# Two spectrum products in one VectorE instruction, and two of seven inverse-stage evictions moved to VectorE

## The chip, the cores and the metric

The kernel runs on one core of a Trainium2 chip. The metric is the device time of one execution in microseconds (us). The core has a matrix engine (TensorE, PE in the profile; its weight loads are PEld), VectorE (DVE), ScalarE (ACT), GpSimd (POOL) and SyncE (SP), which here only issues DMAs. All engines run their own instruction lists in order and meet through semaphores.

## The reference, cut to what matters

The input is a sequence batch x of shape (8, 5696, 128) and a filter h of shape (5696, 128). First comes a causal long convolution along the sequence, done through a Fourier transform of twice the length; then a mixing block over tokens and channels.

```
L = 2 * S
Yf = np.fft.rfft(x, n=L, axis=1) * np.fft.rfft(h, n=L, axis=0)[None]
y = np.fft.irfft(Yf, n=L, axis=1)[:, :S]
theta = y @ w_theta
z = (y * cos(theta), y * sin(theta))
u = y + y_from(w_tok_r, z[0]) + y_from(w_tok_i, z[1])
out = u + relu(u @ w_ch)
```

The change touches only the convolution.

## The kernel before, in words

The convolution occupies the first fifth of the execution; the token mixing, two 5696 x 5696 matrices against the rotated values, fills the rest and keeps TensorE busy almost without a gap (line 1099).

A transform of length 11392 is split into 64 x 178 points, of which 90 columns are kept because the input is real. The work is cut into eight groups, four pairs of batches times two halves of 64 channels. A group passes through four stages.

- **Stage a** (`stage_a`, matmul on line 194) makes the 90 columns in 16 steps; ScalarE evicts each step from PSUM (line 201; 128 x 720).
- **Stage b** (`stage_b`) goes over the 90 columns in 12 chunks, eleven of 8 columns and one of 2. For a chunk, `f2` does 32 short matmuls into a PSUM tile (line 212), ScalarE evicts it as the spectrum tile `xs` (line 310; 128 x 1024), and VectorE multiplies `xs` by the two rows of the filter's spectrum `hs`, one instruction for each (line 312), into `u_t` and `v_t`. The pool of `xs` has two buffers, so the eviction of chunk c waits until the products of chunk c-2 have read theirs. The tile `hs` of chunk c comes from DRAM in two DMAs on SP's queue (line 303); the pool has four buffers, and the loads of chunk c+4 are issued behind the products of chunk c (`LEAD = 4`). The last chunk's PSUM tile also takes 12 wide matmuls that only keep TensorE busy (line 218).
- **Stage c** (`stage_c`) is matmuls of `u_t` and `v_t` against two small tables (lines 328 and 329), which need all chunks of stage b; VectorE (line 336) and for some steps ScalarE (lines 333 and 334) evict them into `g`.
- **Stage d** (`stage_d`) is the last inverse transform: seven steps of up to ten columns, 20 matmuls for a full step (line 351), each evicted by ScalarE into `yt` (line 354; 128 x 890, the last one 128 x 356). Its first step needs all of `g`. At its end `yt` goes to DRAM.

The order of the work is written by hand with `woven`, which merges lists of steps by fractional positions. Two stretches alternate. In one, stage c of a group is woven with stage a of the next. In the other, stage b of the next group is woven with stage d of this one; I call it the **b/d stretch**, and there are seven of it. Its order of steps is b0 d0 b1 b2 d1 b3 b4 d2 b5 b6 d3 b7 d4 b8 b9 d5 b10 b11 d6. In front of the seven there is one stage b without a stage d (about 68 to 88 us), woven with the building of a table, and behind them one stage d without a stage b (about 422 to 438 us), woven with the first steps of the mixing part (`phase_step`), which use ScalarE for sines. All convolution matmuls share a pool of four PSUM tiles, so TensorE can be at most four steps ahead of the evictions. Four steps of the following stage a stand on TensorE between the end of a b/d stretch and the first matmul of stage c. A scheduler places the instructions of each engine; with one exception, noted with the change, it keeps the written order around here.

Of the kernel before, what the change touches and what calls it, by code (L numbers as in the profile page):

```python
# [12 lines left out]
F16 = mybir.dt.float16  # L13
add = mybir.AluOpType.add
mult = mybir.AluOpType.mult
AF = mybir.ActivationFunctionType
# [6 lines left out]
def kernel(  # L23
# [10 lines left out]
    nc = tc.nc  # L34
    B, S, D = x.shape
    assert D == 128
    P = 128
# [42 lines left out]
    K1 = N1 // 2 + 1  # L80
    CK = 8
    HD = D // 2
# [5 lines left out]
    CN = 10  # L88
    CHN = [(c0, min(CN, N2 - c0)) for c0 in range(0, N2, CN)]
    UVW = 2 * HD * K1  # L90
# [6 lines left out]
    def psum():  # L97
        return fp.tile([P, 2, 512], F32, tag="ps", name="ps")
# [3 lines left out]
    def pool(name, bufs, stack, **kw):  # L102
        return stack.enter_context(tc.tile_pool(name=name, bufs=bufs, **kw))
# [6 lines left out]
    fc = pool("fft_c", 1, conv, side="right")  # L110
# [1 line left out]
    s1 = pool("set_1", 1, setup, side="right")  # L112
    s2 = pool("set_2", 2, setup, side="right")

    u_t = fc.tile([P, UVW + P], F16)
    v_t = fc.tile([P, UVW + P], F16)
    uv = [t[:, :UVW].rearrange("p (e d k) -> p e d k", e=2, k=K1) for t in (u_t, v_t)]
    h16 = s1.tile([P, 2, N2, HD], F16)
    for p0, p1 in ((0, 80), (80, NB)):
        nc.gpsimd.dma_start(u_t[p0:p1, :N2 * D],  # L120
# [22 lines left out]
    def turns_of(pattern, base, lanes, m, per, quarter=None):  # L143

        n = 1
        for _, c in pattern:
            n *= c
        t = s2.tile([P, 11 * NB], F32, tag="turn", name="turn")[:m, :n]
        k = s2.tile([P, 11 * NB], F32, tag="whole", name="whole")[:m, :n]
        nc.gpsimd.iota(k, pattern=pattern, base=base, channel_multiplier=0,  # L150
                       allow_small_or_imprecise_dtypes=True)
        nc.gpsimd.tensor_scalar(t, k, lanes, 1.0 / per, op0=mult, op1=mult)
        if quarter is not None:
            quarter(t)
        nc.vector.tensor_scalar(k, t, MAGIC, None, op0=add)
        nc.vector.scalar_tensor_tensor(t, k, MAGIC, t, op0=ALU.subtract, op1=ALU.subtract)
        return t, k
# [12 lines left out]
    t, k = turns_of([[1, K1]], 0, lane[:NB, 1:2], NB, N1)  # L170
# [33 lines left out]
    def f2(a_st, c):  # L204

        c0, ck = CHK[c]
        ps = psum()
        for j in range(ck):
            for ri in range(2):
                for e in range(2):  # L210
                    rows = slice(64 * e, 64 * e + 64)
                    nc.tensor.matmul(ps[:, e, j * HD:(j + 1) * HD],  # L212
                                     w_t2[rows, c0 + j, N2 * (1 - ri):N2 * (3 - ri)],
                                     a_st["a"][rows, ri * K1 + c0 + j, :],
                                     start=(ri == 0), stop=(ri == 1))
        if c == NCK - 1:
            for n in range(WARM):
                nc.tensor.matmul(ps[:, n % 2, ck * HD:ck * HD + 384], w_t2[:, 2, :P],
                                 w_t2[:, 0:2, :].rearrange("p k n -> p (k n)"), start=True, stop=True)
        return ps[:, :, :ck * HD].rearrange("p e (k d) -> p e d k", k=ck)  # L220
# [73 lines left out]
    def stage_b(a_st, dh):  # L294

        hs_of = {}

        def load(c):
            if c >= NCK:
                return  # L300
            hs = hs_of[c] = fh.tile([P, 2, HD * CK], F16, tag="hs", name="hs")
            for e in range(2):
                nc.sync.dma_start(hs[64 * e:64 * e + 64], hf_hbm[dh, c])

        def chunk(c):
            c0, ck = CHK[c]
            hv = hs_of[c].rearrange("p r (d k) -> p r d k", k=CK)
            ps = f2(a_st, c)
            xs = fs.tile([P, 2, HD, CK], F16, tag="xs", name="xs")
            nc.scalar.activation(xs[:, :, :, :ck], ps, AF.Copy)  # L310
            for r in range(2):
                nc.vector.tensor_tensor(  # L312
                    uv[r][:, :, :, c0:c0 + ck], xs[:, :, :, :ck],
                    hv[:, r:r + 1, :, :ck].to_broadcast([P, 2, HD, ck]), op=mult)
            load(c + LEAD)
        return [lambda c=c: load(c) for c in range(LEAD)], [lambda c=c: chunk(c) for c in range(NCK)]

# [21 lines left out]
    def stage_d(st, bp, dh, then=None):  # L339
        def chunk(n0, cn):  # L340
            if n0 == 0:
                st["yt"] = fg.tile([P, NB, N2], BF16, tag="yt", name="yt")
            g_, yt = st["g"], st["yt"]
            ps = psum()
            nq = 5 if cn == CN else cn
            for j in range(cn):
                n = n0 + j
                o = ps[:, j // nq, (j % nq) * NB:(j % nq + 1) * NB]
                for ri in range(2):
                    e_ = e_t[:K1, n, ri, :] if n < EN else e_t[:K1, N2 - n, ri, ::-1]  # L350
                    nc.tensor.matmul(o, g_[:K1, ri * N2 + n, :], e_, start=(ri == 0), stop=(ri == 1))
            y_out = yt[:, :, n0:n0 + cn].rearrange("p m (a q) -> p m a q", q=nq)
            y_in = ps[:, :cn // nq, :nq * NB].rearrange("p a (q m) -> p m a q", q=nq)
            nc.scalar.activation(y_out, y_in, AF.Copy)
            if n0 + cn == N2:
                if then is not None:
                    then(yt)
                if then is not None:
                    gate = nc.gpsimd.tensor_copy(small(0, 1)[HD:HD + 1], sides["phases"][1][HD:HD + 1, 3, H - 1:H]).ins
                for e in range(2):  # L360
                    t0 = H if then else 0
                    with tc.issue_after(gate) if then else ExitStack():
                        (nc.gpsimd if then else nc.sync).dma_start(
                            yt_hbm[dh * HD:(dh + 1) * HD, 2 * bp + e, t0:],
                            yt[64 * e:64 * e + 64].rearrange("p m n -> p (m n)")[:, t0:])
        return [lambda n0=n0, cn=cn: chunk(n0, cn) for n0, cn in CHN]
# [125 lines left out]
    def small(at, n):  # L492
        return ring["all"][:, WB + BT + at:WB + BT + at + n]
# [436 lines left out]
    for i, (k, p, tt, j0, s0, nj) in enumerate(stretches):  # L930
# [38 lines left out]
        if tt is None:  # L969
# [24 lines left out]
            if end_of_pair:  # L994
# [5 lines left out]
                c, c0 = c_last  # L1000
# [161 lines left out]
```

## Time and profile before

| what | us |
|---|---|
| three timed runs, median (lowest to highest) | 2102.5 (2101.66 to 2104.44) |
| the profiled execution, its own time | 2099.89 |
| span of the profiled execution | 2098.1 |
| TensorE busy / VectorE busy / ScalarE busy in the span | 1979.5 / 1595.2 / 675.3 |
| mean granted TensorE clock | 0.978 |
| start of the first spectrum eviction in the seven b/d stretches | 111.05, 153.10, 195.88, 238.35, 281.18, 325.06, 369.11 |

The time of an execution is a little longer than its span, which runs from the first to the last recorded instruction (1.8 us here). Rows of the profile give start and duration of an instruction or of a merged run of equal ones; square brackets give the idle time of the engine before it and what ended that. Instructions that stand back to back overlap a little in the records, so what one costs its engine is the distance from start to start (its slot), not its duration.

### The profile page before, as it was taken

The page shows a single profiled execution, that of the slowest core. Times are in us where ns is not written, and L with a number is a line of the kernel's source. Part 1 is how long each engine was busy: PE and PEld are TensorE (multiplying, and loading weights), DVE is VectorE, ACT ScalarE, POOL GpSimd, SP SyncE. Part 2 cuts the span into 40 slices and gives each one's busy share as a digit, 9 for nine tenths or more (in the row PEclk, how much of TensorE's full clock was granted, in tenths as well). Part 3 has the DMA queues.
Part 4 walks back from the last instruction along what each step waited for, and adds up shares of the span by engine and source line. Part 5 has one row for each costly group of instructions (what it writes and reads, how often), then busy time and mean ns, then how long its engine had stood idle before and what let it go on. Part 6 is the DMA issues. An engine that isn't in the chain of part 4 may idle for free.

```text
span 2098.1 us, 41505 instructions
## 1 busy us (share of the span) xinstructions
PE 1979.5 (94%) x15688; PEld 1109.4 (53%) x15865; DVE 1595.2 (76%) x2881; ACT 675.3 (32%) x995; POOL 912.5 (43%) x1662
## 2 busy tenths in 40 slices
PE   4888999878999999999999999899999999999998
PEld 3788888754444444444444444344444444444444
DVE  7777776776878888888886766886777777777867
ACT  5887877874332333333310000011111111111111
POOL 5301010327444636354557554435354545445450
PEclk8799999989999999999999999999999999999999
DMA  7357474989989989898999989869797887879693
GB/s 144 94 137 175 123 171 121 239 243 239 179 153 179 178 175 168 171 173 177 171 175 152 154 167 284 136 107 156 127 154 132 148 142 136 154 130 155 126 155 89
DMA packets 408233, 334.97 MB, mean 160 GB/s; under 512 B 85895, under 2 KB 358407, under 8 KB 407047
## 3 DMA queue, kind: packets, MB, share of 16 engines
q0 software_dynamic: 225952, 156.72, 52.8%
q1 hardware_dynamic: 176096, 164.05, 27.3%
q10 hardware_dynamic: 5984, 11.54, 1.6%
q8 instruction: 124, 2.03, 0.4%
q14 instruction: 77, 0.63, 0.1%
HBM read 377.11 MB, written 92.49 MB: 224 GB/s over the span
## 4 chain that ended last, share of the span: by engine, by line
PE 63%; DVE 4%; DMA 2%; issue 2%; POOL 0%; ACT 0%; DVEq 0%
PE m L1099 59%; DVE c L1106 2%; DMA ring<-in_moe_w_tok_r_dram 1%; DVE b L655 1%; PE v L801 1%; PE utp L794 1%; PE m L1103 1%; DVE wt L714 1%; PE tpz L742 0%; PE theta_ps L396 0%; POOL ring L509 0%; PE m L986 0%; DMA yT<-yt_hbm 0%; PE m L1020 0%; DMA zl<-zl_hbm 0%
## 5 line engine op out<-in xcount | busy, mean ns | idle before, releaser
L509 POOL DMA_DIRECT2D ring<-in_moe_w_tok_i_dram x720 | 390.8, 557 | 653.0 <-DVE wt L714 579.6
L509 POOL DMA_DIRECT2D ring<-in_moe_w_tok_r_dram x720 | 389.0, 559 | 145.8 <-DVE wt L714 85.5
L714 DVE STREAM_TRANSPOSE wt<-ring 128x384 f32<-128x384 f32 (+2 forms) x720 | 359.3, 523 | 110.3 <-PE m L1099 70.0
L1099 PE MATMUL m<-b,wt 128*128 128x512 bf16 x1599 | 385.9, 380 | 4.1 <-DVE wt L714 1.7
L1099 PEld LDWEIGHTS <-wt 128*128 128x128 bf16 x1804 | 176.4, 98 | 219.7 <-DVE wt L714 7.8
L1106 DVE TENSOR_TENSOR c<-c,m 128x512 f32<-128x512 f32 x412 | 265.2, 669 | 0.4 <-PE m L1099 0.4
L796 ACT ACTIVATE ring<-utp 128x512 bf16<-128x512 bf16 x85 | 50.8, 597 | 582.3 <-PE utp L794 582.3
L328 PE MATMUL ps<-r_u,u_t 128*128 128x128 f16 x1024 | 126.4, 223 | 6.4 <-ACT red L419 3.0
L329 PE MATMUL ps<-r_v,v_t 128*128 128x128 f16 x1024 | 125.5, 223 | 0.4
L1020 PE MATMUL m<-b,wt 128*128 128x512 bf16 x466 | 110.2, 381 | 8.9 <-DMA b<-z_hbm 4.9
L791 ACT ACTIVATE ub<-c 128x512 bf16<-128x512 f32 x88 | 55.0, 628 | 191.5 <-DMA ring<-in_moe_w_tok_r_dram 113.0
L130 POOL DMA_DIRECT2D x<-in_x_dram x64 | 33.9, 536 | 184.9 <-PE ps L194 174.8
L328 PEld LDWEIGHTS <-u_t 128*128 128x128 f16 x1024 | 103.4, 101 | 5.5 <-DVE u_t L312 4.6
L329 PEld LDWEIGHTS <-v_t 128*128 128x128 f16 x1024 | 102.4, 100 | 4.4 <-issue 2.4
L310 ACT ACTIVATE xs<-ps 128x1024 f16<-128x1024 f32 x96 | 96.6, 1030 | 14.7 <-DVE v_t L312 6.7
L312 DVE TENSOR_TENSOR u_t<-xs,hs 128x1024 f16<-128x1024 f16 x96 | 68.6, 715 | 29.2 <-ACT xs L310 19.0
L1020 PEld LDWEIGHTS <-wt 128*128 128x128 bf16 x528 | 51.1, 99 | 69.2 <-issue 9.6
L194 PE MATMUL ps<-f_t,x 89*128 89x180 f16 x512 | 77.2, 298 | 4.0 <-ACT xs L310 2.6
L212 PEld LDWEIGHTS <-w_t 64*128 64x128 f16 x3240 | 60.8, 102 | 37.5 <-issue 24.5
L398 ACT ACTIVATE red<-theta_ps,magic 128x512 f32<-128x512 f32 (+1 forms) x46 | 31.6, 687 | 134.6 <-PE theta_ps L396 104.5
L194 PEld LDWEIGHTS <-x 89*128 89x128 f16 x512 | 70.8, 241 | 5.5 <-issue 4.5
L744 ACT ACTIVATE ring<-tpz 128x512 bf16<-128x512 bf16 (+1 forms) x46 | 27.5, 597 | 131.9 <-PE tpz L742 113.0
(2895 smaller groups left out, 3868.9 us busy)
## 6 DMA issues: line engine op xcount, KB each, us to landing
ring<-in_moe_w_tok_r_dram POOLq DMA_DIRECT2D x352, 96.0 KB, 4.5
ring<-in_moe_w_tok_i_dram POOLq DMA_DIRECT2D x352, 96.0 KB, 4.9
ring<-in_moe_w_tok_r_dram POOLq DMA_DIRECT2D x352, 80.0 KB, 4.5
ring<-in_moe_w_tok_i_dram POOLq DMA_DIRECT2D x352, 80.0 KB, 3.9
hs<-hf_hbm SPq DMA_DIRECT2D x192, 128.0 KB, 3.1
cp_hbm<-c SPq DMA_DIRECT2D x88, 256.0 KB, 2.5
c<-cp_hbm SPq DMA_DIRECT2D x88, 256.0 KB, 4.4
out_dram<-c SPq DMA_DIRECT2D x88, 256.0 KB, 4.5
```

Of the source, the lines that this page charges most:

```text
L194: nc.tensor.matmul(ps[:, i // 2, (i % 2) * 2 * K1:(i % 2 + 1) * 2 * K1], lhs(q + i), f1_t[:NB], start=True, stop=True)
L212: nc.tensor.matmul(ps[:, e, j * HD:(j + 1) * HD], w_t2[rows, c0 + j, N2 * (1 - ri):N2 * (3 - ri)], a_st["a"][rows, ri * K1 + c0 + j, :], s ...
L310: nc.scalar.activation(xs[:, :, :, :ck], ps, AF.Copy)
L312: nc.vector.tensor_tensor(uv[r][:, :, :, c0:c0 + ck], xs[:, :, :, :ck], hv[:, r:r + 1, :, :ck].to_broadcast([P, 2, HD, ck]), op=mult)
L328: nc.tensor.matmul(o, u_t[:, at:at + P], r_u, start=True, stop=False)
L329: nc.tensor.matmul(o, v_t[:, at:at + P], r_v, start=False, stop=True)
L509: nc.gpsimd.dma_start(wb[32 * i:32 * i + 32, :ng, :nj * 64], bass.AP(tensor=a.tensor, offset=a.offset + row0 * S + p * H + i * QR + j0 * 6 ...
L714: nc.vector.transpose(wt.rearrange("p j t r -> p (j t r)").bitcast(F32).rearrange("p (j g t) -> p g j t", j=TJ, g=4)[:, :ng, :nj], wb[:, : ...
L791: nc.scalar.activation(ub[:m].rearrange("p b d -> p (b d)"), c[:m], AF.Copy)
L1020: nc.tensor.matmul(ms[n // 2 * 2 + h], a[n][:, j, :, r], bts_of[p][jj][n % 2 * 2 + h][:, r, :], start=(n % 2 == 0 and jj == 0 and r == 0), ...
L1099: nc.tensor.matmul(ms[q], a[q][:, j, :, r], bts[jj][q][:, r, :], start=(jj == 0 and r == 0), stop=(jj == NJ - 1 and r == 1 and q not in left))
L1106: nc.vector.tensor_tensor(c, z, ms[q], op=op)
```

## The change

The tiles `u_t` and `v_t` become the two parts of one tile `uv_t`. For the eleven full chunks the two products become one instruction over 128 x 2 x 1024 elements: `xs` is repeated over the two parts, each row of `hs` over the two halves of the chunk. The chunk of 2 columns keeps its two instructions. In stage d, steps 1 and 4 of 0 to 6 are evicted by VectorE instead of ScalarE.

```
-    u_t = fc.tile([P, UVW + P], F16)
-    v_t = fc.tile([P, UVW + P], F16)
-    uv = [t[:, :UVW].rearrange("p (e d k) -> p e d k", e=2, k=K1) for t in (u_t, v_t)]
+    uv_t = fc.tile([P, 2, UVW + P], F16)
+    u_t, v_t = uv_t[:, 0], uv_t[:, 1]
+    uv = uv_t[:, :, :UVW].rearrange("p r (e d k) -> p r e d k", e=2, k=K1)
...
-            for r in range(2):
+            if ck == CK:
                 nc.vector.tensor_tensor(
-                    uv[r][:, :, :, c0:c0 + ck], xs[:, :, :, :ck],
-                    hv[:, r:r + 1, :, :ck].to_broadcast([P, 2, HD, ck]), op=mult)
+                    uv[:, :, :, :, c0:c0 + ck], xs.unsqueeze(1).to_broadcast([P, 2, 2, HD, ck]),
+                    hv.unsqueeze(2).to_broadcast([P, 2, 2, HD, ck]), op=mult)
+            else:
+                for r in range(2):
+                    nc.vector.tensor_tensor(
+                        uv[:, r, :, :, c0:c0 + ck], xs[:, :, :, :ck],
+                        hv[:, r:r + 1, :, :ck].to_broadcast([P, 2, HD, ck]), op=mult)
             load(c + LEAD)
...
-            nc.scalar.activation(y_out, y_in, AF.Copy)
+            if n0 // CN in (1, 4):
+                nc.vector.tensor_copy(y_out, y_in)
+            else:
+                nc.scalar.activation(y_out, y_in, AF.Copy)
```

In the built program the order on TensorE and on SP's queue within the convolution is the same as before. In a b/d stretch ScalarE's order loses the two evictions and is otherwise unchanged. VectorE's order is: products of chunks 0 and 1, eviction of step d1, products of chunks 2 to 6, eviction of step d4, products of chunks 7 to 11. The eviction of d1 is thus ahead of the product of chunk 2, although the written order has b2 ahead of d1. In the last stage d the two moved evictions stand between VectorE's products of the mixing part.

## The prediction

> **What bounds the kernel now.** I read the busy shares first, then the stretches of the convolution, then VectorE and ScalarE in one stretch in order of time, then the waits.
>
> ```profile
> PE 1979.5 (94%) x15688; PEld 1109.4 (53%) x15865; DVE 1595.2 (76%) x2881; ACT 675.3 (32%) x995; POOL 912.5 (43%) x1662
> ```
>
> TensorE is the bound of the whole. That is an average; the change sits in the b/d stretches, so here are three of them alone (the columns are stretch, its length, then busy us of PE, PEld, DVE, ACT and POOL, the granted clock, DMA share and GB/s):
>
> ```profile
> 153.20:173.00 19.80, 16.47 (x484) 14.45 (x484) 16.34 (x24) 18.12 (x22) 0.00 (x0) 1.00 0.46 137
> 238.50:258.00 19.50, 16.67 (x484) 14.56 (x484) 15.87 (x24) 17.95 (x21) 0.00 (x0) 1.00 0.47 133
> 325.00:344.00 19.00, 15.51 (x478) 13.67 (x479) 14.72 (x23) 16.50 (x19) 0.00 (x0) 1.00 0.44 128
> ```
>
> Here TensorE has 3 us of slack at full clock, ScalarE is the fullest and VectorE comes close behind. The stretch ends, and stage c begins, when VectorE's last product is done: in the second stretch the last one runs from 173.00 to 173.39 and the first matmul of stage c starts at 173.15. So what counts is how the chain ScalarE - VectorE runs, not which column is fullest. VectorE in that stretch:
>
> ```profile
> 156.80 0.70 DVE L312 TENSOR_TENSOR u_t<-xs,hs 128x1024 f16<-128x1024 f16 x1 [1.34 <-ACT xs L310]
> 157.41 0.69 DVE L312 TENSOR_TENSOR v_t<-xs,hs 128x1024 f16<-128x1024 f16 x1
> 158.01 0.69 DVE L312 TENSOR_TENSOR u_t<-xs,hs 128x1024 f16<-128x1024 f16 x1
> ...
> 167.25 0.69 DVE L312 TENSOR_TENSOR u_t<-xs,hs 128x1024 f16<-128x1024 f16 x1 [1.08 <-DMA hs<-hf_hbm]
> ```
>
> A product has a slot of 0.60 to 0.61, a pair 1.21. The last row shows the second thing that holds VectorE: the filter's spectrum, loaded only after the product four chunks earlier. The waits over 60 to 440 us (total, times, longest) put these side by side:
>
> ```profile
> DVE u_t L312 <- ACT xs L310: 19.0, 28, 1.3
> DVE u_t L312 <- DMA hs<-hf_hbm: 8.4, 11, 1.5
> ACT xs L310 <- DVE v_t L312: 6.7, 15, 1.6
> ```
>
> The third line matters most: ScalarE also waits for VectorE, through the two `xs` buffers. The two engines drive each other.
>
> **Part one, the joined products.** Two slots of 0.605 become one longer one. For f32 from PSUM the copies of 720 elements (0.895) and 1024 elements (1.215, line 246) give 1.05 ns an element and a fixed 0.14. At half that rate 1024 elements take 0.54 + 0.15 = 0.69, which is the product's row, so I read the product as running at twice that rate, and 2048 elements take 0.605 + 0.54 = 1.14. Bounds: the 128 x 256 products (slot 0.30) give a slope of 0.40 ns an element, so 1.01; no gain gives 1.21. I take 1.14, nearest to the same engine at the same rate. Saved: 0.07 a chunk, 0.8 us in eleven chunks. The price of losing the double rate is a rival below. Loads and the reuse of `xs` waited for the second product already, so the joint one frees them 0.07 earlier and no more.
>
> **Part two, the moved evictions.** ScalarE sheds two slots of 0.80, 1.6 us a stretch. VectorE gains two: 0.895 plus 170 elements at 1.05 ns is 1.07, slot 0.99, together 2.0. No row has VectorE evicting this shape; the bounds are 0.81 (720 elements) and 1.14 (1024 elements), and I take the interpolated 0.99. VectorE thus has 1.2 us more work per stretch than before.
>
> [...]
>
> **The chain of one stretch.** Times are us after the start of the first spectrum eviction (153.10 in the stretch shown). Before, from rows: the products of chunks 1, 2, 3, 4, 5 start at 3.70, 4.91, 6.33, 7.54, 9.09 (second stretch), and, in the sixth, where no DMA wait falls there, chunk 6 at 10.29 and chunk 8 at 13.44; the eviction of chunk 10 starts at 15.13 there, which puts its product at 16.2. After, step by step with spectrum slot 0.90 (1.03 to its end), product end 1.22 after its start, and 0.03 and 0.12 of hand-over to VectorE and back:
> - Chunk 1 stays at 3.70 (its eviction stands behind d0's, still on ScalarE). d1's eviction comes next on VectorE, at 4.84: its matmuls end at about 3.74.
> - Chunk 2 goes to 5.83 (0.92 late), chunk 3 to 6.97.
> - The spectrum of chunk 4 needs chunk 2's buffer: 5.83 + 1.22 + 0.12 = 7.17, product 8.23 (0.7 late). ScalarE stands idle here; the slot that it was spared is lost.
> - d2's eviction at 8.07, chunk 5's spectrum at 8.87, product at 9.93 (0.84 late); chunk 6 at 11.07.
> - d4's eviction on VectorE at 12.21, then chunks 7, 8, 9 at 13.20, 14.34 and 15.48. Chunk 8 is 0.9 late.
> - Chunk 9's spectrum needs chunk 7's buffer (14.54), then d5's eviction at 15.44, chunk 10's spectrum at 16.24, product at 17.30.
>
> So chunk 10 is 1.1 late where no load is late. Behind it things stay: the last products run beside stage a's first matmuls (line 194) in both versions and are slow beside them (1.90 instead of 0.69 at 170.28).
> - Against that stand the loads. The second DMA of a chunk is issued 0.6 us behind the first (median of the issue rows) and lands 3.1 us later (median): about 3.7 behind the product that frees the buffer, 5.0 with that product, and more when one is late. Products four chunks apart start 5.4 to 5.9 apart before, 5.2 to 6.2 after. Some late loads (8.4 us in all, 1.2 a stretch) will be covered by the slower pace, up to 0.4 a stretch I estimate.
>
> I take +0.9 a stretch, between +0.7 and +1.1; seven times, +6.3. The other ends: a product of 1.01 takes about 0.6 off a stretch (ten products, half of them covered by other waits), one of 1.21 adds 0.3: +1 to +10 in all.
>
> **Outside the seven.** The first stage b has only the joined products: -0.2 (0 to -0.8). In the last stage d ScalarE is without idle time from 429.8 to 446.9, so one moved eviction (0.79) is worth its slot, the other (before 428.15, where ScalarE waits 0.54 for VectorE) less; VectorE, busy 20.6 of 29.0 us there, pays 2.0. I take -0.5 (+0.5 to -1.6). What follows is a chain on TensorE and through data of the convolution, so it moves along.
>
> Sum: 6.3 - 0.2 - 0.5 = **+5.6 us** on the profiled execution's own time, 2099.9 to 2105.5. That execution is 2.6 below the median shown; on the median the forecast is 2108.1, rounded 2108.
>
> **Rivals.**
> - *ScalarE sets the pace (faster).* It is the fullest engine in each stretch shown, and 1.6 us are taken from it. If VectorE's new slots fall into its idle time (1.34 before chunk 1, 1.08 before chunk 8), 1.2 a stretch is gained, with the last stage -9.6: 2093. It decides if d1's and d4's evictions do not delay the next spectrum, that is if buffer waits (6.7 us in total now) stay few. Against it: d1's eviction can't start before its matmuls end, when the 1.34 gap is over.
> - *The loads hold both versions.* If late loads fall where VectorE's evictions now stand, the evictions are free and the stretch keeps its length: 0 to +0.3 each, about +1: 2103.
> - *The joined product loses its rate.* At f32's 1.05 ns, 2048 elements take 2.28, 1.07 a chunk more; 88 chunks, some 20 of it hidden: +75, 2178. Its operands keep 16 bits and unit steps inside, as before; only outer repeats change.
>
> **How the numbers follow.** Forecast 0.50 (+1 to +10 us), loads 0.30 (-2 to +4), ScalarE 0.16 (-13 to -4), lost rate 0.04. This kernel's measurement tells about 0.2%, 4.2 us, from no change. Of the forecast's case 0.45 lies over +4.2 and 0.05 within; of the loads' 0.02 over and 0.28 within; of ScalarE's 0.01 within, 0.15 below. Slower is 0.45 + 0.02 + 0.04 = 0.51, same 0.34, faster 0.15. The range leaves out the lost rate and the far part of ScalarE's case: 2095 to 2115; the likeliest case alone is 2103 to 2113.
>
> **What would show it.** Right: joined products with a slot near 1.14; VectorE's evictions near 1.07; ScalarE idle before the spectra of chunks 4 and 10, released by VectorE; stretches about 0.9 longer from first spectrum to stage c. Wrong: stretches shorter, few buffer waits of ScalarE, or products near 2.2.

## The result, and the profile after

| | before | after |
|---|---|---|
| median of 22 runs each, us (lowest to highest) | 2100.13 (2096.52 to 2105.53) | 2105.30 (2100.21 to 2115.21) |
| span of the profiled execution, us | 2098.1 | 2105.6 |

The ratio after to before is 1.0025, with a 95% interval of 1.0013 to 1.0036: the change costs 5.2 us (2.7 to 7.6). The forecast was +5.6.

The busy shares of the changed kernel (first line of the profile's page) say little by themselves. VectorE gained 10.2 us and ScalarE lost 12.6:

```profile
PE 1982.7 (94%) x15688; PEld 1112.7 (53%) x15865; DVE 1605.4 (76%) x2809; ACT 662.7 (31%) x979; POOL 907.9 (43%) x1662
```

The same three b/d stretches as before (columns as in the prediction's table of stretches; each starts at its first spectrum eviction and ends at about the first matmul of stage c; the windows in the prediction's table end 0.1, 0.4 and 1.6 us ahead of that matmul, so the lengths of the two tables cannot be compared, only what fills them):

```profile
156.40:177.20 20.80, 16.27 (x484) 14.48 (x484) 17.73 (x16) 17.19 (x20) 0.00 (x0) 1.00 0.43 130
243.00:263.50 20.50, 16.19 (x484) 14.41 (x484) 17.61 (x16) 17.04 (x20) 0.00 (x0) 1.00 0.45 131
329.40:350.00 20.60, 16.25 (x484) 14.47 (x484) 17.66 (x16) 16.95 (x20) 0.00 (x0) 0.99 0.44 130
```

TensorE is about as busy as it was, ScalarE is no longer the fullest engine, and yet a stretch takes longer (20.84, 20.55 and 20.66 us up to that matmul, against 20.04, 20.09 and 20.49). Neither VectorE nor ScalarE is full; each waits for the other. VectorE in the second stretch, whose first spectrum eviction starts at 156.39:

```profile
160.13 1.23 DVE L312 TENSOR_TENSOR uv_t<-xs,hs 128x2048 f16<-128x2048 f16 x1 [1.46 <-ACT xs L310]
161.27 1.08 DVE L360 CAST yt<-ps 128x890 bf16<-128x890 f32 x1
162.26 3.59 DVE L312 TENSOR_TENSOR uv_t<-xs,hs 128x2048 f16<-128x2048 f16 x3
166.65 2.36 DVE L312 TENSOR_TENSOR uv_t<-xs,hs 128x2048 f16<-128x2048 f16 x2 [0.80 <-DMA hs<-hf_hbm]
168.93 1.08 DVE L360 CAST yt<-ps 128x890 bf16<-128x890 f32 x1
169.92 4.15 DVE L312 TENSOR_TENSOR uv_t<-xs,hs 128x2048 f16<-128x2048 f16 x3
174.44 2.43 DVE L312 TENSOR_TENSOR uv_t<-xs,hs 128x2048 f16<-128x2048 f16 x1 [0.37 <-ACT xs L310]
```

Two slots can be read off: a joined product takes 1.14 (160.13 to 161.27), an eviction of stage d on VectorE 0.99 (161.27 to 162.26). The second row is d1's eviction: it stands where, before, the product of chunk 2 stood. ScalarE in the same stretch:

```profile
159.07 1.94 ACT L310 ACTIVATE xs<-ps 128x1024 f16<-128x1024 f32 x2
161.45 1.02 ACT L310 ACTIVATE xs<-ps 128x1024 f16<-128x1024 f32 x1 [0.44 <-DVE uv_t L312]
163.57 1.02 ACT L310 ACTIVATE xs<-ps 128x1024 f16<-128x1024 f32 x1 [1.10 <-PE ps L212]
...
171.23 1.02 ACT L310 ACTIVATE xs<-ps 128x1024 f16<-128x1024 f32 x1 [1.10 <-DVE uv_t L312]
```

The third row is the spectrum of chunk 4, 1.10 late. The profile names TensorE as its releaser, and that needs a second look: TensorE's rows put the matmuls of chunk 4 into this run, done at 161.21:

```profile
160.10 1.11 PE L212 MATMUL ps<-a__2352,w_t 64*128 64x64 f16 x64
```

What ends just ahead of 163.57 is the product of chunk 2, from 162.26 to 163.49; it holds the `xs` buffer that chunk 4 needs. So the wait is on VectorE, and a total by releaser counts too little of it. Taken from the rows alone, ScalarE's idle time ahead of a spectrum (median of the seven stretches) is 0.44 for chunk 3, 1.10 for chunk 4 and 0.99 for chunk 9; before it was 0.01 or less for all three.

The waits over 109 to 390 us, the seven stretches with the stages c between them (total, times, longest), first of before and then of after:

```profile
DVE u_t L312 <- DMA hs<-hf_hbm: 8.4, 11, 1.5
...
ACT xs L310 <- DVE v_t L312: 4.5, 9, 1.6
```

```profile
ACT xs L310 <- DVE uv_t L312: 11.8, 17, 1.1
...
DVE uv_t L312 <- DMA hs<-hf_hbm: 2.3, 5, 0.8
```

One kind of wait took the place of another: VectorE waits 6.1 us less for the filter's spectrum, and ScalarE at least 7.3 us more for VectorE.

**How the stretches are compared below.** "Length" is from the first spectrum eviction to the first matmul of stage c. The granted clock is not 1.00 everywhere: it falls to half for periods of 3.4 us or a multiple (3.41, 6.83, 10.24 and 17.07 us up to 440 us in the profile of before), and where they fall differs from one execution to the next. They seldom hit the stretches 2, 4 and 6 (in one stretch of e2 by 6.8 us, otherwise by 0.7 us or less), so I use the mean of these three, the **quiet mean**: 20.21 us before, 20.68 after. It comes from one profiled execution per kernel and says nothing of the other four stretches. The three lengths of one kernel spread by up to 1.2 us (by 0.3 or less in after, e6, e7 and e9). Differences of 0.2 or less between quiet means are not told apart, and between kernels with a wide spread a difference counts only if all three stretches show it.

Most expectations below are for the sum of all seven stretches (142.6 us before, 146.7 after). These sums take in the periods at half clock, 7.3 us in the stretches of before and 17.5 in those of after, so that a sum can miss its range for that alone.

### The profile page after: what moved, and what is told of

Same layout as the page of the kernel before. It is cut to its first block, busy times and chain, and to the rows that moved or that the text cites. A ratio compares the mean times of both kernels' runs of the same rounds, so it can differ in the third digit from the quotient of the medians.

```text
span 2105.6 us, 41427 instructions
## 1 busy us (share of the span) xinstructions
PE 1982.7 (94%) x15688; PEld 1112.7 (53%) x15865; DVE 1605.4 (76%) x2809; ACT 662.7 (31%) x979; POOL 907.9 (43%) x1662
## 4 chain that ended last, share of the span: by engine, by line
PE 63%; DVE 4%; DMA 3%; issue 1%; POOL 1%; ACT 0%; DVEq 0%; ACTq 0%; SPq 0%; POOLq 0%
PE m L1107 59%; DVE c L1114 1%; DVE b L663 1%; DMA ring<-in_moe_w_tok_r_dram 1%; PE utp L802 1%; PE v L809 1%; DMA b<-z_hbm 1%; PE m L1111 1%; DVE wt L722 1%; POOL ring L517 1%; PE theta_ps L404 0%; PE tpz L750 0%; DMA yT<-yt_hbm 0%; PE m L994 0%; PE m L1028 0%
## 5 line engine op out<-in xcount | busy, mean ns | idle before, releaser
L333 PE MATMUL ps<-r_u,uv_t 128*128 128x128 f16 x1024 | 127.7, 225 | 9.4 <-DVE uv_t L317 5.9
L312 DVE TENSOR_TENSOR uv_t<-xs,hs 128x2048 f16<-128x2048 f16 x88 | 115.1, 1334 | 23.9 <-ACT xs L310 19.9
L334 PE MATMUL ps<-r_v,uv_t 128*128 128x128 f16 x1024 | 126.8, 225 | 0.4
L333 PEld LDWEIGHTS <-uv_t 128*128 128x128 f16 x1024 | 104.1, 102 | 7.5 <-DVE uv_t L317 7.0
L334 PEld LDWEIGHTS <-uv_t 128*128 128x128 f16 x1024 | 103.2, 101 | 5.6 <-issue 3.5
```

Source lines behind the costliest of these rows:

```text
L312: nc.vector.tensor_tensor(uv[:, :, :, :, c0:c0 + ck], xs.unsqueeze(1).to_broadcast([P, 2, 2, HD, ck]), hv.unsqueeze(2).to_broadcast([P, 2, ...
L333: nc.tensor.matmul(o, u_t[:, at:at + P], r_u, start=True, stop=False)
L334: nc.tensor.matmul(o, v_t[:, at:at + P], r_v, start=False, stop=True)
```

## The experiments

The theory: the loss is that of the two moved evictions. They delay the products behind them, so these hold the two `xs` buffers longer, and ScalarE stands idle; the joined products are a small gain; late loads of the filter's spectrum, which before held VectorE, hide part of the loss. The rivals: the joined products lose; VectorE's longer sum of work is what counts, wherever it stands; or the loads set the pace of both kernels.

| run | what it is | median, us (before beside it) | ratio, 95% interval | quiet mean, us |
|---|---|---|---|---|
| e1_joined | joined products alone | 2100.84 (2102.48) | 0.9991, 0.9981 to 1.0000 | 20.10 |
| e2_moved | moved evictions alone | 2109.65 (2102.48) | 1.0031, 1.0018 to 1.0043 | 21.18 |
| e3_after_xs3 | after, three `xs` buffers | 2104.96 (2102.48) | 1.0006, 0.9993 to 1.0019 | 20.58 |
| e4_joined_d0 | joined, step 0 moved in place of 1 and 4 | 2100.83 (2102.48) | 0.9989, 0.9977 to 1.0002 | 19.67 |
| e6_before_hs5 | before, five `hs` buffers | 2099.03 (2102.05) | 0.9985, 0.9974 to 0.9997 | 19.35 |
| e7_after_hs5 | after, five `hs` buffers | 2106.39 (2102.05) | 1.0014, 1.0000 to 1.0028 | 20.63 |
| e8_joined_d0_hs5 | e4 with five `hs` buffers | 2098.55 (2102.05) | 0.9981, 0.9970 to 0.9992 | 19.26 |
| e9_after_xs3_hs5 | after, three `xs`, five `hs` | 2101.55 (2102.05) | 0.9994, 0.9983 to 1.0006 | 19.43 |
| e10_joined_d1 | joined, step 1 alone moved | 2106.22 (2101.96), one run | none | 20.69 |
| e11_joined_d4 | joined, step 4 alone moved | 2100.93 (2101.96), one run | none | 20.25 |
| e12_before_a_late | before, stage a woven later | 2110.75 (2101.96), one run | none | 18.71 |

The last three were run once; they are judged by their stretches, not by their times.

### The two parts by themselves

e1 has the first hunks of the diff and leaves all evictions on ScalarE. e2 keeps the two products per chunk and has only the last hunk.

> The joined products alone, all seven evictions of stage d on ScalarE. Measure: the sum of the seven b/d stretches, from the first spectrum eviction to the first matmul of stage c (142.6 us before, 146.7 after the change). Theory (the moved evictions delay the products, and through the two spectrum buffers ScalarE): shorter than before, 139.5 to 142, time -0.5 to -3 us, because a chunk's products take 1.14 instead of 1.21. Rival (the joined instruction itself is the delay, since it gives both halves late): longer than before, 144 to 147.

> The two moved evictions alone, products in two instructions as before. Theory: longer than after the change, since nothing is given back: sum of the seven stretches 147 to 152, time +5 to +10 us against before. Rival (joined products are the delay): 141 to 143, as before or shorter, for ScalarE is relieved of 1.6 us a stretch.

The parts have opposite signs: the joined products alone give -1.9 us by the ratio (-4.0 to 0), the moved evictions alone +6.5 (+3.8 to +9.0). Their sum, +4.6, is that of the change within its interval. One of e2's three quiet stretches had 6.8 us at half clock and is 21.88 long; the other two are 20.81 and 20.85. The 12 runs of e2 also had a lower granted clock than the 35 of before beside them (0.974 against 0.979 in the mean), so a part of the 6.5 can be time at half clock; whether the longer stretches bring that about was not tried.

The sums of the seven stretches are 149.5 in e2, as expected, and 144.3 in e1, which is outside the expected 139.5 to 142 and inside the rival's range. In that profile 17.1 us at half clock fell into the stretches, against 7.3 in before. The quiet stretches, without any, are 19.49, 20.48 and 20.33, neither all longer nor all shorter than before. What speaks against the rival is the time.

The waits over 109 to 390 us agree, first e1 and then e2:

```profile
ACT xs L310 <- DVE uv_t L312: 3.7, 5, 1.4
```

```profile
ACT xs L310 <- DVE v_t L312: 17.8, 21, 1.2
```

Before had 4.5, so ScalarE's waits for VectorE grow only where the evictions moved. A cost of the joined product is ruled out as far as the time tells: the interval of e1 ends at 1.0000.

### Which of the two evictions

```
-            if n0 // CN in (1, 4):
+            if n0 == CN:          # e10; e11: n0 == 4 * CN; e4: n0 == 0
```

> The joined products with one moved eviction, that of step 1 (it stands between the products of chunks 1 and 2). The theory: the two moved evictions cost through the chain of two evicted-spectrum buffers, and the first of them does most of it, since VectorE has no gap at that place and the spectrum of chunk 4 then waits for the buffer of chunk 2: mean of the stretches 2, 4 and 6 about 20.5 us, and ScalarE's waits for VectorE's product about as many as in the changed kernel (10 us or more in the seven stretches). The rival, that it is VectorE's longer sum of work that costs, each moved eviction the same: half of the way from the joined products alone (20.10) to the changed kernel (20.68), 20.4, here and with step 4 alone.

> The joined products with one moved eviction, that of step 4 (it stands between the products of chunks 6 and 7). The theory: it falls at a place where the product of chunk 7 is late for its spectrum-buffer load in the kernel before anyway, so that it costs little: mean of the stretches 2, 4 and 6 about 20.2 us, and ScalarE's waits for VectorE about those of the joined products alone (4 to 7 us). The rival, each moved eviction the same: 20.4, as with step 1 alone.

> Joined products, and instead of steps 1 and 4 step 0 of stage d is evicted by VectorE, where VectorE stands idle before chunk 1 (1.34 us). Theory: that eviction is free on VectorE and lets the spectrum of chunk 1 start some 0.2 us earlier: sum of the seven stretches 138 to 141.5, time -1 to -4 us against before. Rival (any eviction on VectorE costs its slot of about 1.0): 1 us a stretch over the joined products alone, 146 to 149.

Step 1 alone gives a quiet mean of 20.69, as long as with both; step 4 alone 20.25, next to 20.10 with neither; step 0 alone 19.67. One and the same eviction of 1.08 us thus costs 0.6 or nothing that can be told, by its place, and VectorE's sum of work does not decide. That step 0 on VectorE gains anything is not shown. Two of its three stretches are as long as in e1 (19.54 and 20.35, against 19.49 and 20.33); the whole difference is in the fourth stretch, 19.14 against 20.48, and there VectorE waits 1.59 for a late load in e1, as its row shows, and 0.72 in e4:

```profile
251.62 5.41 DVE L312 TENSOR_TENSOR uv_t<-xs,hs 128x2048 f16<-128x2048 f16 x3 [1.59 <-DMA hs<-hf_hbm]
```

The times do not tell the two apart either (0.9989 and 0.9991). The sum of e4, 140.7, is in its range.

The waits by releaser missed what was expected of them (7.9 us in e10, 10.6 in e11). In e10 that is the fault of naming shown above; the idle time from the rows is clear: ScalarE idles 0.44 ahead of chunk 3 and 1.10 ahead of chunk 4 (medians), just as in after. In e11 the expectation itself was wrong: ScalarE idles 0.50 ahead of chunk 8 and 1.09 ahead of chunk 9. ScalarE in the second stretch of each, first e10 (the spectrum of chunk 4), then e11 (of chunk 9):

```profile
163.74 1.02 ACT L310 ACTIVATE xs<-ps 128x1024 f16<-128x1024 f32 x1 [1.10 <-PE ps L212]
```

```profile
166.05 1.02 ACT L310 ACTIVATE xs<-ps 128x1024 f16<-128x1024 f32 x1 [1.09 <-DVE uv_t L312]
```

So step 4 does make ScalarE wait, but near the end of the stretch: ahead of chunk 11's spectrum ScalarE idles 0.92 in e1 and 0.14 in e11, and I read that gap as what takes the delay up. Step 0's eviction falls into the gap of VectorE ahead of the product of chunk 1, which then starts at 3.52 instead of 3.74 in the median.

### Taking away ScalarE's wait

```
-    fs = pool("fft_s", 2, conv, side="right")
+    fs = pool("fft_s", 3, conv, side="right")
```

The third buffer takes 2 KB a partition, given by the mixing part's buffers `zz` (three to two here and in the runs with five `hs` buffers, one in e9). Fewer `zz` buffers alone were not run, so what they do to the whole time is not known.

> The changed kernel with three spectrum buffers instead of two; for the room, the mixing part's pool zz has two buffers instead of three, which touches nothing in the first six stretches. Theory (the chain through the spectrum buffers carries the delay): ScalarE's waits for VectorE's products (13.0 us after, 6.7 before) fall below 5, and the seven stretches sum to 143 to 145.5. Rival (VectorE simply has more work): waits of ScalarE fall as well but VectorE is the pace: sum 146 to 147.5.

ScalarE no longer stands still for chunks 3 and 4: four spectra run back to back, as this row of ScalarE in e3's second stretch shows (its first spectrum eviction starts at 154.21).

```profile
156.90 3.76 ACT L310 ACTIVATE xs<-ps 128x1024 f16<-128x1024 f32 x4
```

The product of chunk 5 starts at 9.28 instead of 10.00 (medians, us after the first spectrum eviction), and ScalarE's waits for VectorE fall from 11.8 us to 4.4, as expected. But the quiet mean gains only 0.1, which cannot be told from nothing, because the next limit is right behind:

```profile
DVE uv_t L312 <- DMA hs<-hf_hbm: 7.0, 10, 1.5
```

With the buffers freed, VectorE waits for loads again, 7.0 us instead of 2.3. The sum of the seven stretches, 144.9, is in its range. The run could not settle the size, only the mechanism, and the loads had to be taken away too.

### Taking away the loads' wait

```
-    fh = pool("fft_h", 4, xa)
+    fh = pool("fft_h", 5, xa)
...
-    LEAD = 4
+    LEAD = 5
```

> The kernel before with five buffers for the filter's spectrum, loaded five chunks ahead instead of four; for the room, the mixing part's pool zz has two buffers instead of three. If late loads hold the old kernel's stretches (8.4 us of waits), these waits nearly vanish and the seven stretches sum to 136 to 140 (142.6 before), time -2 to -6 us. If ScalarE's pace holds them, the sum stays at 141 to 143.

> The changed kernel with the same fifth buffer. Theory (the chain through the two spectrum buffers sets the pace after the change, loads hardly wait there: 2.3 us in the seven stretches): the start of chunk 5 stays near 10.0 us after the first spectrum, sum 143 to 146.5, so the distance to the kernel before with the fifth buffer grows from 4.1 to 5 to 9 us. Rival (loads are the pace of both): sum 139 to 142, distance under 3.

The fifth buffer makes a quiet stretch of before 0.86 shorter (20.21 to 19.35), and of after 0.05 (20.68 to 20.63). In both runs the list of waits has none left for the filter's spectrum. What is left in e7 is the other wait, as large as in after:

```profile
ACT xs L310 <- DVE uv_t L312: 12.6, 16, 1.1
```

So in these stretches the old kernel was held by its loads, the new one is held by the `xs` buffers, and without late loads the change costs 1.28 a stretch (20.63 less 19.35; 1.21, 1.33 and 1.28 one by one), against 0.47 with them. That the loads hold both kernels is ruled out there.

Over the seven stretches the picture is weaker. The sums are 140.6 for e6, between the two ranges that were given, and 143.5 for e7, in its range; their distance is 2.9, not 5 to 9, and by that mark the rival's. Half-clock periods are in it (10.3 us in e6, 6.8 in e7), but the seventh stretch, which has none in either run, also differs by 0.52 only (19.81 less 19.29). In the whole time the pair differs by 6.1 us by the ratios, 0.9 a stretch, against 5.2 with four buffers. So the 1.28 is the cost in the stretches 2, 4 and 6, and that the cost of the whole grows when the loads are early is not shown.

> The changed kernel with three spectrum buffers and five for the filter's spectrum; the mixing part's pool zz keeps one buffer, so the total is not compared, only the stretches. Theory (two things hold the changed kernel, the spectrum buffers and behind them the loads; three spectrum buffers alone gave 144.9, with 7.0 us of waits for loads): sum 137 to 141. Rival (VectorE has too much work): 143 to 146.

With both waits taken away, the changed kernel's quiet mean is 19.43, against 19.35 for before with five buffers (the sum, 140.4, is in its range). The change then costs nothing that can be told in these stretches; it also gains nothing, although ScalarE does 1.6 us less in a stretch. Before with a third `xs` buffer as well was not run; in e6 the list of waits has none of ScalarE for VectorE, so there was little for that buffer to take away.

### A version that beats both

> Joined products, step 0 of stage d on VectorE, and the fifth buffer: what the runs so far point to. Theory: both gains add, seven stretches 133 to 138 (140.7 with four buffers), time -5 to -10 us against the kernel before. Rival (another bound, TensorE's own 14 to 16 us or its half-clock stretches, comes up): 138 to 141, time -1 to -4.

Joined products, the eviction of step 0 alone on VectorE, five `hs` buffers: 0.9981 of before (0.9970 to 0.9992), 4.0 us faster. Against the changed kernel's 1.0025 the intervals are far apart. Most of it comes with the fifth buffer (and the `zz` buffer given for it): e6 has 0.9985. That the other two edits add to it is not shown, and the expectation that both gains add was missed: the sum of the stretches is 139.7, not 133 to 138, and the time 4.0 us shorter, not 5 to 10. Both lie in the rival's ranges; 10.8 us at half clock are in the sum, and no run tells whether TensorE is the bound that the rival names. A stretch is 0.95 shorter in the quiet mean, which would be 6.7 us over seven; the time shows 4.0 (1.7 to 6.3).

### The slow products at the end of a stretch

```
-        woven((c_, 0.06 if a_ else 0.0, 1.0), (a_, 0.0, 0.35 if dh == 0 else 0.55), now, load_)
+        woven((c_, 0.0, 1.0), (a_, 0.1, 0.45 if dh == 0 else 0.65), now, load_)
```

> The kernel before, with the next group's stage a woven into stage c from 0.1 on instead of from its start, so that stage c's own first matmuls stand ahead of stage a's, and no weight load of stage a runs beside the last products of stage b. If those strided weight loads slow the products and the evictions beside them: the last products of a stretch take their usual 0.69 us instead of 1.9, the last spectrum eviction 1.03 instead of 1.6, the stretches to the first matmul of stage c are 1.5 to 2 us shorter, and stage c is longer by the steps moved into it. If the products are slow for another reason (their place at the end of the stretch, the loads of weights for stage c), they stay at 1.9 and the stretch loses only what the moved steps took on TensorE.

Before, the last products of the second stretch run beside stage a's first matmuls (line 194). VectorE and then TensorE:

```profile
168.46 1.29 DVE L312 TENSOR_TENSOR u_t<-xs,hs 128x1024 f16<-128x1024 f16 x1
169.06 1.24 DVE L312 TENSOR_TENSOR v_t<-xs,hs 128x1024 f16<-128x1024 f16 x1
170.28 1.90 DVE L312 TENSOR_TENSOR u_t<-xs,hs 128x1024 f16<-128x1024 f16 x1
```

```profile
169.08 0.71 PE L194 MATMUL ps<-f_t,x 89*128 89x180 f16 x4
170.30 0.62 PE L194 MATMUL ps<-f_t,x 89*128 89x180 f16 x4 [0.51 <-ACT xs L310]
171.15 1.12 PE L194 MATMUL ps<-f_t,x 89*128 89x180 f16 x8 [0.23 <-ACT xs L310]
```

In e12 the first matmul of stage a in that stretch stands at 176.53, behind the last full product, and the products take their usual time:

```profile
174.10 0.69 DVE L312 TENSOR_TENSOR v_t<-xs,hs 128x1024 f16<-128x1024 f16 x1
174.75 0.69 DVE L312 TENSOR_TENSOR u_t<-xs,hs 128x1024 f16<-128x1024 f16 x1
175.36 0.68 DVE L312 TENSOR_TENSOR v_t<-xs,hs 128x1024 f16<-128x1024 f16 x1
```

All seven stretches of e12 are so, and the quiet mean falls by 1.5 to 18.71. It is no way to a faster kernel as it stands: the moved steps lengthen the seven stages c by 13.3 us together (157.9 to 171.2). I read this as time that they had filled before, in which TensorE waits for the last products.

## Why the prediction was right, and where it was not

- **The mechanism was right.** "The spectrum of chunk 4 needs chunk 2's buffer" is what the rows of after show and what the third buffer takes away in e3. The chain was right to less than a tenth up to chunk 6: predicted starts of the products of chunks 2 to 6 were 5.83, 6.97, 8.23, 9.93, 11.07, the medians are 5.88, 7.01, 8.25, 10.00, 11.14. For chunks 7 and 8 the chain, drawn without late loads, had 13.20 and 14.34; after has 13.53 and 14.67, e7, where no load is late, 13.24 and 14.37. Chunk 10 was drawn at 17.30 and came at 18.33 (17.90 in e7); the rows from there on are lengthened beside stage a (2.43 instead of 1.23 at 174.44). One time of the chain does not fit the others: chunk 9's product was put at 15.48, before its own spectrum, started at 14.54 and 1.03 long, was there; e7 has 15.60.
- **The durations were right**: a slot of 1.14 for the joined product and of 0.99 for VectorE's eviction, as predicted, and 1.08 for the eviction's length where 1.07 was. "The joined product loses its rate" is ruled out by these rows and by e1.
- **The mis-sized term is the cover by the loads**: "up to 0.4 a stretch I estimate". In the quiet stretches it is 0.8, the distance without late loads (1.28) less the one with them (0.47), so the term "+0.9 a stretch" is too large there. The 1.1 drawn for a stretch without late loads stands against 1.28, near enough. The reason given was right ("late loads will be covered by the slower pace"); I saw that the old kernel waits 1.2 us a stretch for loads and took a third of it off, where the waits fell by 6.1 of 8.4. For the other four stretches the size of the cover is open (6.1 us without late loads and 5.2 with them in the whole time).
- **Where ScalarE idles** was half right: named were the spectra of chunks 4 and 10; it is chunk 4 and chunk 9, where the chain itself had drawn a wait too, and 0.44 ahead of chunk 3, which was not foreseen. The chain had 0.8 of its 1.1 in place by chunk 6, ahead of the second moved eviction; what that one was to add does not show in the quiet mean (20.69 with step 1 alone, 20.68 with both).
- **Outside the seven**: the first stage b became 0.55 shorter (predicted 0.2), and between the last start of stage c and the mixing's first matmul 1.4 were gained (predicted 0.5). Both errors are on the side of the gain, but less time at half clock fell into both in after (9.6 us instead of 14.3, and 9.5 instead of 13.4), so they are not the change's alone.
- **The sum was right partly by chance.** In the profiled pair the seven stretches give +4.1 instead of +6.3; the stages c in front of them, which the change does not touch, give +2.0; at the start of the mixing after is 4.1 late, after its first pass 5.2, and the whole span 7.5. At half clock were 17.5 us in the stretches of after and 7.3 in those of before, and 22.6 against 16.6 in the stages c. The +2.0 goes with that: the four stages c whose time at half clock differs give +2.2 together, the three where it is equal differ by less than 0.1 each. How much of the +4.1 is the clock's is not known, nor whether the change brings more such periods (the mean granted clock is 0.978 over the 22 runs of after, 0.979 and 0.980 over two sets of 35 of before). How the last 2 us come about, at the change of passes and behind it, is not settled: it is a single pair of executions, and in the medians the whole is 5.2. The parts as measured do not add up to the 5.2: the quiet mean's 0.47 over seven stretches is 3.3, and the gains outside come off it.
- The predicted time of 2108.0 stood on the median of the first three runs, 2102.5; over 22 runs before has 2100.1. Of the 2.7 by which the time is under the forecast, 2.4 are this.

## What to carry to other kernels

Two engines that hand tiles to each other through two buffers are one loop: work given to the second engine ahead of a product delays the first engine two tiles later (here by 1.10 ahead of chunk 4's spectrum), even if the first is the fuller one and is the one relieved. Choose the place by the order of time, and not by the sums of busy time: in the gap ahead of chunk 1 (step 0) the eviction costs nothing that can be told, ahead of chunk 2 (step 1) it costs 0.6 a stretch. Before sizing a loss or a gain, ask which other wait is only just behind, and take that one away in both kernels: in the quiet stretches a fifth load buffer showed a cost of 1.28 that the plain comparison had as 0.47. And check such a figure against the whole time, which here did not show that growth.

## What the runs showed of the hardware

- **Stage a's matmuls slow VectorE and ScalarE.** Beside them, in the second stretch of before, a product takes up to 1.90 instead of 0.69 and a spectrum eviction 1.59 instead of 1.03 (at 168.66); GpSimd had no instruction in that stretch (0.00 us busy), and in e12, with the matmuls elsewhere, they are back to 0.69 and to 1.02 to 1.09. Stage a's weight loads are also slow themselves, 238 ns in the median for 89x128, where those of lines 328 and 351 take 98. What in stage a's steps holds the two engines up was not tried.
- **The clock falls to half inside the convolution.** Two stages c of the kernel before, without and with such a period (columns as in the stretches; the clock is the third number from the end):

```profile
131.10:153.00 21.90, 21.84 (x340) 21.49 (x340) 14.91 (x13) 17.93 (x23) 0.00 (x0) 1.00 0.37 98
173.20:195.80 22.60, 22.51 (x336) 22.05 (x336) 14.60 (x13) 14.45 (x22) 8.30 (x16) 0.92 0.81 172
```

  In the twelve profiles other than e12's, a stage c without such a period takes 21.7 to 22.0 us (34 of them), one with 3.2 to 3.8 us at half clock 22.5 to 23.5 (41), and one with 5.8 to 6.5 us 23.4 to 23.6 (9). Of the 74 periods that begin between 109 and 390 us in the thirteen profiles, 66 follow 3.4 us in which TensorE was busy less than 70% of the time, and none follows over 80%. Other stretches of 3.4 us with less than 70% had none behind them (the one up to 119.8 in before, with 60%), and ahead of 109 us one begins behind 96% (at 61.8 in before), so what sets a period off is not shown. The same stage c can thus differ by 1.35 us between two profiles (22.04 in before with none, 23.39 in after with one), as much as the largest cost of the change in a quiet stretch (1.33, e7 less e6).
